# Retention and a gated MLP on one Trainium2 core: outputs of three chunks in two PSUM banks, a pair of first ups, other pieces of w_in, a w_out cast on GpSimd

## The chip, the core and the metric

One NeuronCore of a Trainium2 chip runs the whole kernel. The metric is device time in microseconds (us) of one execution; the number given is the median of several runs. Engines are named as the profile names them: PE is TensorE (matmuls), PEld its weight loads, DVE is VectorE, ACT is ScalarE, POOL is GpSimd, SP is SyncE, whose queue here only issues DMAs. Every engine works through its own instructions strictly in the order in which they are written; they wait for each other by semaphores.

## What is computed

```python
# q, k, v: 8 batches x 8 heads x 576 rows x 64, f32;  gamma of a head: 1 - 2^(-5-h)
scores = scale * q @ k.T                       # 576 x 576 per batch and head
ret = scores * where(i >= j, gamma**(i-j), 0)  # causal, decaying
attn = ret @ v                                 # retention, no softmax
x = attn.transpose(0, 2, 1, 3).reshape(4608, 512)
h = x @ w_in                                   # 512 x 2048
g = h * 1/(1 + exp(-beta*h))                   # beta per column of h
out = g @ w_out                                # 2048 x 512, f32
```

## The kernel before

**Retention in chunks.** The decay factors into a gain on q and a gain on k or v, so that rows are worked in chunks: 512 rows of a batch make four chunks of 128 (`seq[i]` gives batch and chunk; batch 0 has i = 0 to 3, batch 1 has 4 to 7), and the 64 rows left over in each batch are worked in pairs at four later places. For each chunk, in bf16: `pre_q` and `pre` scale and cast q, k and v (on DVE for the first two batches' q, else on POOL); `t_q` and `t_k` transpose them on PE through PSUM tiles `T` and copy them out (`qT`, `kT`); `a_sc` makes the scores of eight heads in two PSUM tiles `sc` and multiplies each by the causal mask on DVE (`R`); `a_O` multiplies `R` with v into the PSUM tile `O`; `a_cross` adds q times the state of the chunks before; `a_x` copies `O` to `xT`, the transposed input of the MLP; `a_st` adds the chunk's k^T v to the state `st` in PSUM and copies it out on ACT in two halves (`sbd`, or `end` after the last chunk). Below, "scores 6" or "T_k6" are those of chunk i = 6.

**The MLP.** A block is the 512 rows of a batch. `up(m, fo)` is four matmuls of 512 columns (one for each 128 rows of w_in, `ko`) into a PSUM tile `ph`, and ACT's Silu into `gT`; sixteen `fo` make a block. For block 1 the first ten are done in halves of 256 columns, since its chunks come two and two: first for chunks 4 and 5, then for 6 and 7. `down(m, ms, f0)` is four matmuls of a group of four `fo` for 128 rows `ms` into a PSUM tile `po`, copied out by DVE (`ot`) after the last group and stored.

**Loads and weights.** All loads stand in SP's queue: q of batch 0, k and v of its chunks, w_in in six pieces (four of 256 columns, two of 512), w_out in four groups, then q, k and v of batch 1, and so on. w_in pieces are cast to bf16 on DVE and POOL (L185, L186), w_out groups are scaled by 1/beta in three casts on DVE and one on ACT (L195 to L200). q of batch 1 arrives in two DMAs; `pre_q` makes four DVE instructions of it.

**Buffers.** PSUM has eight banks, given out by tag in turn: `mm` three (`ph`, `po`, the second `t_q`), `sc` two, `O` two (also `T`), `st` one. A tile waits until the one that had its bank has been read. For the fourth 128 rows of block 0, `po` takes the bank of the first rows' `po`, which the first `ot` copy releases.

**Order.** Nothing is scheduled by a compiler; the order of the program is each engine's order. Batch 0's chunks are written out by hand (L457 to L497). Then `merged` (L443) goes through `fill`, a list of ups and downs, and before unit n issues every step of `streams` whose due number is n or less. In block 0, `fill` has 16 ups, then (`d0` = 16) downs: twelve with `f0` outer and three `ms` inner, four for the last `ms`; `u1` = `d0` + 16 is block 1's first up. `second(i)` is `a_O` of two chunks, `a_cross` of both, `a_x` of both, and `a_st` of the second.

Of the kernel before, what the change touches and what calls it, by code (L numbers as in the profile page):

```python
# [19 lines left out]
def kernel(  # L20
# [110 lines left out]
    for h in range(H):  # L131
# [41 lines left out]
    def load_w_in(g):  # L173
        f0, fn = pieces[g]
        if f0 % 512 == 0:
            whole[0] = stage.tile([P, KO, 512], F32, name="wt", tag="wt", bufs=4)
        t = whole[0][:, :, f0 % 512:f0 % 512 + fn]
        nc.sync.dma_start(t, w_in_r[:, :, f0:f0 + fn])  # L178
        wts[g] = t

    def cast_w_in(g, kos=range(KO)):
        t = wts[g]
        f0, fn = pieces[g]
        for ko in kos:
            on_pool = ko == KO - 1 or g < 4 and ko > 1  # L185
            (nc.gpsimd if on_pool else nc.vector).tensor_copy(w_in_sb[:, ko, f0:f0 + fn], t[:, ko])  # L186
# [119 lines left out]
    def q_cols(i, r, p):  # L306

        b, c = seq[i]
        if b is None:
            return live[i]["qkT"][r, 0, p, :], lambda o: o  # L310
        return (batch[b]["qT"][r, :, p, c * PC:(c + 1) * PC], lambda o: o.rearrange("k (i s) -> k i s", i=CB))

    def a_sc(i):
        L = live[i]
        L["R"] = R = sb.tile([P, 2, HP, P], BF16, name="R", tag="R", bufs=4)

        tag = "mm" if i == CB - 1 else "O" if i >= E and (i - E) % 2 else "sc"
        sc = [psum.tile([P, HP, P], F32, name="sc", tag=tag, bufs=3 if tag == "mm" else 2) for _ in range(2)]
        for p in range(HP):
            for j in range(2):  # L320
                r = slice(j * D, (j + 1) * D)
                rhs, view = q_cols(i, r, p)
                nc.tensor.matmul(view(sc[j][:, p, :]), L["kT"][r, p, :], rhs, start=True, stop=True,  # L323
                                 skip_group_check=True)
        mask = causal if seq[i][0] is not None else causal2
        m_b = mask[:].unsqueeze(1).to_broadcast([P, HP, P])
        if i == CB - 1:

            half = sb.tile([P, HP, P], BF16, name="half", tag="half", bufs=1)
            nc.scalar.copy(half[:], sc[1][:])  # L330
            sc[1] = half
        for j in range(2):
            nc.vector.tensor_tensor(R[:, j], sc[j][:], causal4[:] if i == CB - 1 else m_b, ALU.mult)  # L333

    def a_cross(i, first):

        b, c = seq[i]
        L = live[i]
        if first:
            L["O"] = psum.tile([P, HP, P], F32, name="O", tag="O", bufs=2)  # L340
        if c == 0 and b is not None:
            return
        for p in range(HP):
            rhs, view = q_cols(i, slice(0, P), p)
            if b is None:
                for x in range(2):
                    r = slice(x * TL, (x + 1) * TL)
                    nc.tensor.matmul(L["O"][:, p, r], ends[(2 * c + x) % 4][:, p, :], rhs[:, r],
                                     start=False, stop=True, skip_group_check=True)
            else:  # L350
                nc.tensor.matmul(view(L["O"][:, p, :]), sbds[(c - 1) % NS][:, p, :], rhs,  # L351
                                 start=first and p == 0, stop=not first, skip_group_check=True)

    def a_O(i):

        b, c = seq[i]
        L = live[i]

        early = i < E
        if not early:  # L360
            tag = "sc" if b is not None and b >= QB and c > 1 else "O"
            L["O"] = psum.tile([P, HP, P], F32, name="O", tag=tag, bufs=2)
        O, R, vn = L["O"], L["R"], L["vn"]
        crossed = b is None or c > 0
        for j, p in [(n // HP, n % HP) if early else (n % 2, n // 2) for n in range(H)]:
            nc.tensor.matmul(O[j * D:(j + 1) * D, p, :], vn[:, 2 * p + j, :], R[:, j, p, :],  # L366
                             start=p == 0 and not (early and crossed), stop=early or not crossed,
                             skip_group_check=True)
        if early:
            a_x(i)  # L370

    def a_x(i):
        b, c = seq[i]
        O = live[i]["O"]
        if b is None:
            x = xt(B)[:, :, c, :]
        else:
            x, O = xt(b)[:, :, :, c * PC:(c + 1) * PC], O.rearrange("k p (i s) -> k p i s", i=CB)
        if i == CB - 1:
            nc.vector.tensor_copy(x[:, :2], O[:, :2])  # L380
            nc.scalar.copy(x[:, 2:], O[:, 2:])
        else:
            on_act = i < E or i % 2 == 0 if i < 2 * E else b is not None and c == 1
            (nc.scalar.copy if on_act else nc.vector.tensor_copy)(x, O[:])  # L384
# [21 lines left out]
    def up(m, fo, c0=0, cn=CB):  # L406
        if m not in gts:
            gts[m] = sb.tile([P, FO, CB, P], BF16, name="gT", tag="gT", bufs=2)
        w = slice(c0 * PC, (c0 + cn) * PC)
        ph = psum.tile([P, CB, P], F32, name="ph", tag="mm", bufs=3)  # L410
        ph = ph.rearrange("f i s -> f (i s)")[:, :cn * P].rearrange("f (i s) -> f i s", i=CB)
        for ko in range(KO):
            nc.tensor.matmul(ph, w_in_sb[:, ko, fo * P:(fo + 1) * P], xts[m][:, ko, :, w],  # L413
                             start=(ko == 0), stop=(ko == KO - 1))
# [38 lines left out]
    def F(f, *a):  # L453
        return lambda: f(*a)
# [66 lines left out]
    def second(i):  # L521
        for f in (a_O, lambda j: a_cross(j, False), a_x):
# [98 lines left out]
```

## Time and profile before

| what | value |
|---|---|
| runs | 311.74, 311.5, 311.76 us; median 311.74 |
| the profiled execution: time, span | 311.92 us, 310.1 us |
| granted TensorE clock | 0.998 of full speed |
| PE from 0 to 20 us | 15.29 us busy |
| PE from 20 to 40 us | 19.51 us busy |
| PE from 40 to 60 us | 19.15 us busy |
| PE from 60 to 250 us | 188.03 us busy |
| PE from 250 us to the end | 56.56 us busy; its last matmul ends at 306.8 |
| first up of block 0, first down, first up of block 1 | 19.48, 34.12, 52.22 us |
| w_in loads, 256 and 512 columns: issue to landing | 7.5 and 11.8 us |

The page of a profile gives busy time by engine, the span in 40 slices, DMA queues, the chain of work that ended last, and the costliest groups of instructions. A line of the timeline reads: start in us from the span's start, time covered, engine, source line, operation, out<-in by the program's names, shape, count, and in brackets how long the engine was idle before and what ended that. A run of equal instructions is merged into one line. A busy PE can still be waiting in part, as the ends of matmuls are modelled.

### The profile page before, as it was taken

Reading aid. Unit: us, or ns where it says so; the run is one execution under the profiler, and the core shown is the slowest. Engines: PE = TensorE matmul, PEld = TensorE weight load, DVE = VectorE, ACT = ScalarE, POOL = GpSimd, SP = SyncE. Lnnn points to the kernel's source line nnn. Section 1 sums busy time; section 2 is a strip of 40 time slices with the busy share of each in tenths; the row PEclk is TensorE's granted clock in tenths of the full one; section 3 lists DMA queues with packets and bytes.
Section 4 is the critical chain, followed back from the end, with each engine's and each line's share of the span. In section 5 each row is a group of like instructions: output and inputs, shape, how many; then the busy total and the mean of one; then the engine's idle time right before and its main releaser. Section 6 shows DMA issues by size and latency. Waiting matters only on the chain.

```text
span 310.1 us, 5363 instructions
## 1 busy us (share of the span) xinstructions
PE 298.5 (96%) x2144; PEld 157.8 (51%) x2177; DVE 106.9 (34%) x191; ACT 143.0 (46%) x256; POOL 96.0 (31%) x131
## 2 busy tenths in 40 slices
PE   7789999999999999999999999999999999999995
PEld 5544456775544454454554545455545444444444
DVE  7554476342531342434430434043405420010012
ACT  5567626995138412560186117711673037207700
POOL 4663026846524282254308031902420000000000
PEclk9999999999999999999999999999999999999999
DMA  8999999998989999999897697968852110031011
GB/s 207 221 355 387 380 232 273 233 257 179 202 197 162 224 189 235 218 212 198 133 234 107 136 205 207 201 115 192 196 76 37 68 70 0 17 88 34 0 70 68
DMA packets 123897, 52.79 MB, mean 170 GB/s; under 512 B 105680, under 2 KB 116320, under 8 KB 123872
## 3 DMA queue, kind: packets, MB, share of 16 engines
q1 hardware_dynamic: 98496, 46.15, 61.5%
q10 hardware_dynamic: 25376, 6.30, 13.6%
q8 instruction: 17, 0.28, 0.4%
q14 instruction: 8, 0.07, 0.1%
HBM read 36.71 MB, written 9.44 MB: 149 GB/s over the span
## 4 chain that ended last, share of the span: by engine, by line
PE 85%; DMA 6%; SPq 5%; DVE 1%; issue 1%; ACT 1%; POOL 1%; POOLq 0%
PE po L426 40%; PE ph L413 35%; DMA wt<-in_moe_w_in_dram 4%; SPq L94 3%; PE O L366 3%; PE sc L323 3%; DMA qn<-in_q_dram 2%; PE O L351 2%; PE st L396 2%; SPq L178 1%; POOL qs L247 1%; PE T L297 1%; PE T L303 1%; ACT gT L415 0%; DVE xT L384 0%
## 5 line engine op out<-in xcount | busy, mean ns | idle before, releaser
L415 ACT ACTIVATE gT<-ph,beta_sb 128x512 bf16<-128x512 f32 (+1 forms) x154 | 99.2, 659 | 86.3 <-PE ph L413 83.4
L413 PE MATMUL ph<-xT,w_in_sb 128*128 128x512 bf16 (+1 forms) x600 | 129.3, 365 | 3.2 <-DVE w_in_sb L186 0.9
L426 PE MATMUL po<-w_out_sb,gT 128*128 128x512 bf16 (+2 forms) x591 | 126.7, 368 | 1.1 <-issue 0.3
L413 PEld LDWEIGHTS <-w_in_sb 128*128 128x128 bf16 x616 | 58.7, 98 | 65.0 <-DVE w_in_sb L186 2.3
L426 PEld LDWEIGHTS <-gT 128*128 128x128 bf16 x608 | 57.1, 98 | 62.5
L333 DVE TENSOR_TENSOR R<-sc,causal 128x512 bf16<-128x512 f32 x71 | 44.3, 684 | 68.9 <-PE sc L323 68.9
L433 DVE COPY ot<-po 128x512 f32<-128x512 f32 (+2 forms) x38 | 25.0, 662 | 92.1 <-PE po L426 92.0
L255 POOL TENSOR_TENSOR vn<-kvn,gv 128x512 bf16<-128x512 f32 x32 | 33.4, 1042 | 22.8 <-DMA kvn<-in_v_dram 11.5
L247 POOL TENSOR_TENSOR qs<-qn,gq 128x512 bf16<-128x512 f32 x24 | 24.3, 1042 | 33.2 <-DMA qn<-in_q_dram 33.2
L273 POOL CAST kn<-kvn 128x512 bf16<-128x512 f32 x32 | 19.6, 612 | 47.7 <-DMA kvn<-in_k_dram 47.3
L401 ACT CAST sbd<-st 64x256 bf16<-64x256 f32 x48 | 17.4, 362 | 15.0 <-PE st L396 14.3
L384 DVE CAST xT<-O 128x512 bf16<-128x512 f32 x24 | 15.8, 688 | 19.6 <-PE O L366 9.6
L384 ACT CAST xT<-O 128x512 bf16<-128x512 f32 x11 | 6.4, 586 | 32.2 <-PE O L351 25.2
L396 PE MATMUL st<-vn,kn 128*128 128x128 bf16 x128 | 12.4, 219 | 0.2 <-POOL vn L255 0.2
L396 PEld LDWEIGHTS <-kn 128*128 128x128 bf16 x128 | 9.3, 98 | 5.0 <-issue 0.2
L366 PE MATMUL O<-R,vn 128*64 128x128 bf16 x288 | 10.7, 221 | 0.0
L323 PE MATMUL sc<-qT,kT 64*128 64x128 bf16 x256 | 10.3, 217 | 0.4 <-ACT kT L304 0.2
L366 PEld LDWEIGHTS <-vn 128*64 128x64 bf16 x288 | 8.5, 110 | 4.1 <-issue 3.6
L323 PEld LDWEIGHTS <-kT 64*128 64x128 bf16 x288 | 8.1, 94 | 3.8 <-ACT kT L304 1.5
L304 ACT COPY kT<-T 128x512 bf16<-128x512 bf16 x12 | 6.9, 586 | 4.8 <-PE T L303 4.8
L208 PE MATMUL ph<-warm 128*128 128x128 f32 (+1 forms) x24 | 7.0, 429 | 1.2 <-DVE warm L119 1.2
L186 DVE CAST w_in_sb<-wt 128x256 bf16<-128x256 f32 (+1 forms) x14 | 6.0, 476 | 5.2 <-DMA wt<-in_moe_w_in_dram 5.2
(56 smaller groups left out, 90.2 us busy)
## 6 DMA issues: line engine op xcount, KB each, us to landing
qn<-in_q_dram SPq DMA_DIRECT2D x16, 512.0 KB, 5.8
kvn<-in_k_dram SPq DMA_DIRECT2D x32, 256.0 KB, 5.9
kvn<-in_v_dram SPq DMA_DIRECT2D x32, 256.0 KB, 5.6
out_dram<-ot SPq DMA_DIRECT2D x31, 256.0 KB, 2.7
wt<-in_moe_w_out_dram SPq DMA_DIRECT2D x4, 1024.0 KB, 9.5
wt<-in_moe_w_in_dram SPq DMA_DIRECT2D x4, 512.0 KB, 7.5
wt<-in_moe_w_in_dram SPq DMA_DIRECT2D x2, 1024.0 KB, 11.8
out_dram<-ot SPq DMA_DIRECT2D x9, 128.0 KB, 2.4
```

The source lines that it names most:

```text
L247: e.tensor_tensor(batch[b]["qs"][:, cs, hs], q_tiles[b][:, hs, cs].rearrange("p h i d -> p i h d"), gq[:, cs, hs].unsqueeze(3).to_broadcas ...
L255: nc.gpsimd.tensor_tensor(live[i]["vn"][:], kv_tiles.pop(i)[:, 1], gains(gv, c), ALU.mult)
L273: nc.gpsimd.tensor_copy(kn[:, c % 2], t[:, 0])
L323: nc.tensor.matmul(view(sc[j][:, p, :]), L["kT"][r, p, :], rhs, start=True, stop=True, skip_group_check=True)
L333: nc.vector.tensor_tensor(R[:, j], sc[j][:], causal4[:] if i == CB - 1 else m_b, ALU.mult)
L366: nc.tensor.matmul(O[j * D:(j + 1) * D, p, :], vn[:, 2 * p + j, :], R[:, j, p, :], start=p == 0 and not (early and crossed), stop=early or ...
L384: (nc.scalar.copy if on_act else nc.vector.tensor_copy)(x, O[:])
L396: nc.tensor.matmul(st[:, p, :], heads(L["kn"], p), heads(L["vn"], p), start=(c == 0 and p == 0), stop=True, skip_group_check=True)
L413: nc.tensor.matmul(ph, w_in_sb[:, ko, fo * P:(fo + 1) * P], xts[m][:, ko, :, w], start=(ko == 0), stop=(ko == KO - 1))
L415: nc.scalar.activation(gts[m][:, fo, :, w], ph, ACT.Silu, scale=beta_sb[:, fo:fo + 1])
L426: nc.tensor.matmul(po[:, :nn], gT[:, fo, ms, :], w_out_sb[:, fo, n0:n0 + nn], start=(fo == 0), stop=(fo == FO - 1))
L433: nc.vector.tensor_copy(ot, po[:, :nn])
```

## The change

- **Two banks.** The output tiles of chunks 3, 5 and 7 become two tiles of half size (heads 0 to 3, heads 4 to 7), each in a bank of its own: chunk 3 in both `sc` banks, chunks 5 and 7 in one `O` and one `sc` bank. DVE copies the first half to `xT`, ACT the second. Before, chunk 3 was copied in halves out of one bank, and chunks 5 and 7 whole by DVE.
- **Chunk 3's products.** The ACT copy `half` of its second score tile goes, and so do `causal4` and its POOL copy; DVE multiplies both tiles from PSUM.
- **Order in batch 0.** `a_sc(3)` comes ahead of `a_cross(2)`, `a_x(1)` behind `t_k(3)`; `a_x` is called on its own.
- **Pieces of w_in.** Six of 256 columns and one of 512. Pieces 0, 1 and the last are loaded in two DMAs of two row groups each. Casts alternate between DVE and POOL by `ko`; in piece 0 POOL takes the first two; in the last piece the second two are cast 256 columns at a time.
- **First ups.** `up_pair` does `fo` 0 and 1 together: `ko` 0 and 1 of both, then `ko` 2 and 3 of each.
- **w_out.** The fourth cast of group 0 moves from ACT to POOL.
- **Due numbers.** Casts and loads of weights follow the new pieces; batch 1's transposes, scores, states and outputs have others.

```diff
-    causal4 = consts.tile([P, HP, P], BF16, name="causal4")
-    nc.gpsimd.tensor_copy(causal4[:], causal[:].unsqueeze(1).to_broadcast([P, HP, P]))
...
-    pieces = [(f, 256) for f in range(0, 1024, 256)] + [(f, 512) for f in range(1024, d_ff, 512)]
+    pieces = [(f, 256) for f in range(0, 1536, 256)] + [(f, 512) for f in range(1536, d_ff, 512)]
...
-        nc.sync.dma_start(t, w_in_r[:, :, f0:f0 + fn])
+        for w in (slice(0, 2), slice(2, KO)) if g in (0, 1, NP - 1) else (slice(0, KO),):
+            nc.sync.dma_start(t[:, w], w_in_r[:, w, f0:f0 + fn])
...
-            on_pool = ko == KO - 1 or g < 4 and ko > 1
-            (nc.gpsimd if on_pool else nc.vector).tensor_copy(w_in_sb[:, ko, f0:f0 + fn], t[:, ko])
+            on_pool = ko < 2 if g == 0 else ko % 2
+            e = nc.gpsimd if on_pool else nc.vector
+            if fn > 256 and ko == 2:
+                for x in range(0, fn, 256):
+                    for o, eng in ((2, nc.vector), (3, nc.gpsimd)):
+                        eng.tensor_copy(w_in_sb[:, o, f0 + x:f0 + x + 256], t[:, o, x:x + 256])
+            elif fn == 256 or ko < 2:
+                e.tensor_copy(w_in_sb[:, ko, f0:f0 + fn], t[:, ko])
...
-            if i == KO - 1:
+            if i == KO - 1 and g == 0:
+                nc.gpsimd.tensor_scalar(w_out_sb[:, fo, :], t[:, i], rbeta_sb[:, fo:fo + 1], None, ALU.mult)
+            elif i == KO - 1:
...
-        if i == CB - 1:
-
-            half = sb.tile([P, HP, P], BF16, name="half", tag="half", bufs=1)
-            nc.scalar.copy(half[:], sc[1][:])
-            sc[1] = half
         for j in range(2):
-            nc.vector.tensor_tensor(R[:, j], sc[j][:], causal4[:] if i == CB - 1 else m_b, ALU.mult)
+            nc.vector.tensor_tensor(R[:, j], sc[j][:], m_b, ALU.mult)
+
+    def split(i):
+        return i in (CB - 1, CB + 1, 2 * CB - 1)
+
+    def new_O(i):
+        b, c = seq[i]
+        if split(i):
+            tags = ("sc", "sc") if i == CB - 1 else ("O", "sc")
+            live[i]["O"] = [psum.tile([P, 2, P], F32, name="O", tag=t, bufs=2) for t in tags]
+        else:
+            tag = "sc" if b is not None and b >= QB and c > 1 else "O"
+            live[i]["O"] = [psum.tile([P, HP, P], F32, name="O", tag=tag, bufs=2)]
...
-        if i == CB - 1:
-            nc.vector.tensor_copy(x[:, :2], O[:, :2])
-            nc.scalar.copy(x[:, 2:], O[:, 2:])
+        Os = live[i]["O"]
+        if split(i):
+            nc.vector.tensor_copy(x[:, :2], view(Os[0]))
+            nc.scalar.copy(x[:, 2:], view(Os[1]))
         else:
-            on_act = i < E or i % 2 == 0 if i < 2 * E else b is not None and c == 1
-            (nc.scalar.copy if on_act else nc.vector.tensor_copy)(x, O[:])
+            on_act = i < 2 * E or b is not None and c == 1
+            (nc.scalar.copy if on_act else nc.vector.tensor_copy)(x, view(Os[0]))
...
+    def up_pair(m, fo, u):
...
+        fs = (fo, fo + 1)
+        if u == 0:
+            for f in fs:
+                phs[f] = psum.tile([P, MB], F32, name="ph", tag="mm", bufs=3)
+        for f, ko in [(f, ko) for ko in (0, 1) for f in fs] if u == 0 else [(f, ko) for f in fs for ko in (2, 3)]:
+            nc.tensor.matmul(phs[f][:], w_in_sb[:, ko, f * P:(f + 1) * P], xts[m][:, ko],
+                             start=(ko == 0), stop=(ko == KO - 1))
+            if ko == KO - 1:
+                nc.scalar.activation(gts[m][:, f], phs[f][:], ACT.Silu, scale=beta_sb[:, f:f + 1])
...
     t_k(3)
+    a_x(1)
     warm_up(1, 128)
+    a_sc(3)
     a_cross(2, True)
-    a_sc(3)
...
-    fill = [F(up, 0, fo) for fo in range(FO)]
+    fill = [F(up_pair, 0, fo, u) for fo in (0,) for u in range(2)] + [F(up, 0, fo) for fo in range(2, FO)]
...
-    streams = [[(0, F(load_w_out, 0)), (1.1, F(cast_w_in, 2)), (3.1, F(cast_w_in, 3)), (3.2, F(load_w_out, 1)),
-                (6.1, F(cast_w_in, 4)), (6.2, F(load_w_out, 2)), (10.1, F(cast_w_in, 5)), (10.2, F(load_w_out, 3))],
+    streams = [[(0, F(load_w_out, 0)), (0.1, F(cast_w_in, 2)), (2.1, F(cast_w_in, 3)), (2.2, F(load_w_out, 1)),
+                (4.1, F(cast_w_in, 4)), (6.1, F(cast_w_in, 5)), (6.2, F(load_w_out, 2)), (8.1, F(cast_w_in, 6)),
+                (8.2, F(load_w_out, 3))],
...
-               [(d0 + 7, F(pre_q, 1, n)) for n in range(4)] + [(d0 + 10.6, F(t_q, 1, 0)), (d0 + 12.6, F(t_q, 1, 1))],
+               [(d0 + 7, F(pre_q, 1, n)) for n in range(4)] + [(d0 + 11.6, F(t_q, 1, 0)), (d0 + 12.6, F(t_q, 1, 1))],
...
-                (d0 + 12.7, F(t_k, 4)), (d0 + 12.8, F(t_k, 5)), (d0 + 13.8, F(a_sc, 4)), (d0 + 13.81, F(a_sc, 5)),
-                (d0 + 14.8, F(a_st, 4)), (d0 + 15.9, F(second, 4))],
+                (d0 + 12.7, F(t_k, 4)), (d0 + 14, F(t_k, 5)), (d0 + 14, F(a_sc, 4)), (d0 + 15, F(a_sc, 5)),
+                (d0 + 15.7, F(a_st, 4)), (d0 + 15.9, F(second, 4))],
...
-                (d0 + 15.8, F(t_k, 6)), (d0 + 15.91, F(t_k, 7)), (u1 + 1.8, F(a_sc, 6)), (u1 + 1.81, F(a_sc, 7)),
-                (u1 + 2.8, F(a_st, 6)), (u1 + 8.8, F(second, 6))]]
+                (d0 + 15.95, F(t_k, 6)), (u1 + 1, F(t_k, 7)), (u1 + 3, F(a_sc, 6)), (u1 + 3.01, F(a_sc, 7)),
+                (u1 + 4, F(a_st, 6)), (u1 + 8.8, F(second, 6))]]
```

More of the change, by code (lines that the diff above doesn't have):

```diff
@@ L326, in a_sc, with O_of, opens @@
         m_b = mask[:].unsqueeze(1).to_broadcast([P, HP, P])
-        if i == CB - 1:
-            half = sb.tile([P, HP, P], BF16, name="half", tag="half", bufs=1)
-            nc.scalar.copy(half[:], sc[1][:])
-            sc[1] = half
         for j in range(2):
-            nc.vector.tensor_tensor(R[:, j], sc[j][:], causal4[:] if i == CB - 1 else m_b, ALU.mult)
+            nc.vector.tensor_tensor(R[:, j], sc[j][:], m_b, ALU.mult)
[9 more added lines that the diff above has]
+            live[i]["O"] = [psum.tile([P, HP, P], F32, name="O", tag=tag, bufs=2)]
+    def O_of(i, p):
+        Os = live[i]["O"]
+        return Os[p // 2][:, p % 2] if split(i) else Os[0][:, p]
+    def opens(i, p):
+        return p == 0 or split(i) and p == 2
     def a_cross(i, first):
         b, c = seq[i]
-        L = live[i]
         if first:
-            L["O"] = psum.tile([P, HP, P], F32, name="O", tag="O", bufs=2)
+            new_O(i)
         if c == 0 and b is not None:
@@ L344, in a_cross @@
             rhs, view = q_cols(i, slice(0, P), p)
+            O = O_of(i, p)
             if b is None:
@@ L347, in a_cross @@
                     r = slice(x * TL, (x + 1) * TL)
-                    nc.tensor.matmul(L["O"][:, p, r], ends[(2 * c + x) % 4][:, p, :], rhs[:, r],
+                    nc.tensor.matmul(O[:, r], ends[(2 * c + x) % 4][:, p, :], rhs[:, r],
                                      start=False, stop=True, skip_group_check=True)
             else:
-                nc.tensor.matmul(view(L["O"][:, p, :]), sbds[(c - 1) % NS][:, p, :], rhs,
-                                 start=first and p == 0, stop=not first, skip_group_check=True)
+                nc.tensor.matmul(view(O), sbds[(c - 1) % NS][:, p, :], rhs,
+                                 start=first and opens(i, p), stop=not first, skip_group_check=True)
     def a_O(i):
@@ L360, in a_O @@
         if not early:
-            tag = "sc" if b is not None and b >= QB and c > 1 else "O"
-            L["O"] = psum.tile([P, HP, P], F32, name="O", tag=tag, bufs=2)
-        O, R, vn = L["O"], L["R"], L["vn"]
+            new_O(i)
+        R, vn = L["R"], L["vn"]
         crossed = b is None or c > 0
         for j, p in [(n // HP, n % HP) if early else (n % 2, n // 2) for n in range(H)]:
-            nc.tensor.matmul(O[j * D:(j + 1) * D, p, :], vn[:, 2 * p + j, :], R[:, j, p, :],
-                             start=p == 0 and not (early and crossed), stop=early or not crossed,
+            nc.tensor.matmul(O_of(i, p)[j * D:(j + 1) * D], vn[:, 2 * p + j, :], R[:, j, p, :],
+                             start=opens(i, p) and not (early and crossed), stop=early or not crossed,
                              skip_group_check=True)
-        if early:
-            a_x(i)
     def a_x(i):
         b, c = seq[i]
-        O = live[i]["O"]
         if b is None:
-            x = xt(B)[:, :, c, :]
+            x, view = xt(B)[:, :, c, :], lambda o: o
         else:
-            x, O = xt(b)[:, :, :, c * PC:(c + 1) * PC], O.rearrange("k p (i s) -> k p i s", i=CB)
-        if i == CB - 1:
-            nc.vector.tensor_copy(x[:, :2], O[:, :2])
-            nc.scalar.copy(x[:, 2:], O[:, 2:])
-        else:
-            on_act = i < E or i % 2 == 0 if i < 2 * E else b is not None and c == 1
-            (nc.scalar.copy if on_act else nc.vector.tensor_copy)(x, O[:])
+            x, view = xt(b)[:, :, :, c * PC:(c + 1) * PC], lambda o: o.rearrange("k p (i s) -> k p i s", i=CB)
+        Os = live[i]["O"]
+        if split(i):
+            nc.vector.tensor_copy(x[:, :2], view(Os[0]))
+            nc.scalar.copy(x[:, 2:], view(Os[1]))
+        else:
+            on_act = i < 2 * E or b is not None and c == 1
+            (nc.scalar.copy if on_act else nc.vector.tensor_copy)(x, view(Os[0]))
     def a_st(i):
@@ L415, in up @@
         nc.scalar.activation(gts[m][:, fo, :, w], ph, ACT.Silu, scale=beta_sb[:, fo:fo + 1])
+    phs = {}
+    def up_pair(m, fo, u):
+        if m not in gts:
+            gts[m] = sb.tile([P, FO, CB, P], BF16, name="gT", tag="gT", bufs=2)
+        fs = (fo, fo + 1)
[7 more added lines that the diff above has]
+                nc.scalar.activation(gts[m][:, f], phs[f][:], ACT.Silu, scale=beta_sb[:, f:f + 1])
     pos_, ots = {}, {}
@@ L474 @@
     a_O(0)
+    a_x(0)
     a_sc(1)
@@ L489 @@
     a_O(2)
+    a_x(2)
     pre(3, (1,))
@@ L493 @@
     a_O(3)
+    a_x(3)
     cast_w_in(0)
```

## Prediction

> **What bounds it now.** I read the page first (busy time, slices), then the timeline from 12 to 66 us, the weights' tiles, and the waits.
>
> ```profile
> span 310.1 us, 5363 instructions
> PE 298.5 (96%) x2144; PEld 157.8 (51%) x2177; DVE 106.9 (34%) x191; ACT 143.0 (46%) x256; POOL 96.0 (31%) x131
> PE   7789999999999999999999999999999999999995
> ACT  5567626995138412560186117711673037207700
> ```
>
> TensorE is busy in all but the first three slices and the last. The diff touches what runs up to about 60 us; past that no instruction changes its place. So the sum is: when does TensorE, now, reach the uninterrupted stretch that begins at 59.44, and when after the change. The waits it could lose there are small; the timeline shows how they hang on loads and on ScalarE:
>
> ```profile
> 18.88 0.80 POOL L186 CAST w_in_sb<-wt 128x256 bf16<-128x256 f32 x2 [1.75 <-DMA wt<-in_moe_w_in_dram]
> 20.35 0.70 DVE L186 CAST w_in_sb<-wt 128x256 bf16<-128x256 f32 x2 [0.53 <-DMA wt<-in_moe_w_in_dram]
> ...
> 26.06 1.51 DVE L186 CAST w_in_sb<-wt 128x512 bf16<-128x512 f32 x3 [2.02 <-DMA wt<-in_moe_w_in_dram]
> ...
> 28.77 1.51 DVE L186 CAST w_in_sb<-wt 128x512 bf16<-128x512 f32 x3 [1.20 <-DMA wt<-in_moe_w_in_dram]
> ...
> 42.66 1.29 DVE L247 TENSOR_TENSOR qs<-qn,gq 128x512 bf16<-128x512 f32 x2 [0.27 <-DMA qn<-in_q_dram]
> ...
> 43.88 1.94 DVE L433 COPY ot<-po 128x512 f32<-128x512 f32 x3
> ...
> 44.06 1.89 PE L426 MATMUL po<-w_out_sb,gT 128*128 128x512 bf16 x8
> ```
>
> To see: every cast starts when its piece lands. A 256-wide piece (512 KB, 1 KB packets) takes 20.35 - 18.88, about 1.49 us; a 512-wide one (1 MB, 2 KB packets) 28.77 - 26.06 = 2.71. Through all of this the slices show the DMA engines at 9 tenths. VectorE's third qs waits for q of batch 1 to land, and the ot copies stand behind qs in VectorE's order.
>
> **Up to 44 us: a gain.** Chunk 3's kT copy goes ahead of x(1) on ScalarE: its transposes end at 14.99, so 15.03 to 15.62 instead of 15.37 to 15.97, and chunk 3's scores start at 15.67 (now 16.02). `half` goes: ScalarE loses 0.58, VectorE's second product reads PSUM, 0.69 instead of 0.41; both products end at 17.41 (now 17.55). Without `half` the state copies run 16.65 to 17.41 (now to 17.72), so the cross product starts at 17.46 instead of 17.77 and everything to chunk 3's output is 0.31 earlier. Its two halves (0.42 on DVE, 0.37 on ACT, one after the other now, 18.59 to 19.42) lie in two banks and run together: 18.28 to 18.70. The first row half of piece 0 lands half a piece earlier, 18.13; GpSimd's two casts (0.4 each) are done by 18.95. First up matmul: 18.76 instead of 19.48. The pair's order needs rows 2 and 3 only at the fifth matmul, so the 0.2 us wait inside the first up goes, and with 256-wide pieces the 0.6 us wait at 26.5 to 27.6 goes. 64 matmuls x 0.216 = 13.82: down starts at 32.6 (now 34.12).
>
> Against it, one 512-wide piece becomes two 256-wide: 2 x 1.49 - 2.71 = **0.27 us later** for every load behind it. Four more DMAs: taken as nothing (the engines never run dry); at most 0.1 from the spread of the 1.49s. w_out then lands at 31.7, 34.4, 37.1, 39.8; its casts cost some 0.4 us of waits in twelve units of 4 x 0.216 = 0.863. GpSimd's w_out cast has no row: bounds 0.61 (its bf16 cast of this size) and 1.04 (its product); I take 0.87, the w_in cast of the same shape. It is wanted at 33.2, lands 31.7, so it is hidden either way; uncovered it costs at most 0.4. Taking its share from ScalarE (0.72) frees nothing that TensorE waits for. With T_q's 0.45 TensorE reaches the first unit of the fourth 128 rows at 43.8, 1.1 us before today's 44.92.
>
> The Trainium skill (GPSIMD Engine Reference, Key points) speaks against GpSimd here: elementwise work is about 2x faster on VectorE, and the two share SBUF interfaces. The rows agree in kind: of the three 128x512 casts from 26.06 on, VectorE's second takes 0.84 beside GpSimd's and its third 0.41 alone. By it VectorE's first w_out casts are 0.4 us later; that falls into the 1.1 us above.
>
> **At 44 us: the gain is lost.** That unit takes the PSUM buffer of the first rows' po, released by the first ot copy, which VectorE does after the fourth qs, whose load lands 0.27 later: 42.93; two qs 0.61 apart, ot 44.14 to 44.83, TensorE at 44.88. Now: ot ends 44.56, TensorE arrives at 44.92. **Net 0.04 earlier**; all the rest of the 1.1 is a new wait there.
>
> **From 44.9 to 61: a loss.**
>
> ```profile
> 49.54 0.76 ACT L401 CAST sbd<-st 64x256 bf16<-64x256 f32 x2 [1.81 <-PE st L396]
> ...
> 50.57 0.58 ACT L304 COPY kT<-T 128x512 bf16<-128x512 bf16 x1 [0.27 <-PE T L303]
> ...
> 51.06 0.59 ACT L384 CAST xT<-O 128x512 bf16<-128x512 f32 x1
> ...
> 51.47 0.69 DVE L384 CAST xT<-O 128x512 bf16<-128x512 f32 x1 [0.32 <-PE O L351]
> ...
> 51.75 0.76 ACT L401 CAST sbd<-st 64x256 bf16<-64x256 f32 x2
> ...
> 52.22 0.77 PEld L413 LDWEIGHTS <-w_in_sb 128*128 128x128 bf16 x8 [0.51 <-DVE xT L384]
> ...
> 52.53 0.58 ACT L304 COPY kT<-T 128x512 bf16<-128x512 bf16 x1
> ...
> 53.20 0.45 PEld L323 LDWEIGHTS <-kT 64*128 64x128 bf16 x16 [0.21 <-issue]
> ```
>
> To see: today ScalarE does chunk 4's state copies and chunk 6's kT while TensorE still has down units; x5 on VectorE costs the weight loads 0.5 us of idle at 52.22. The change puts a_st(4) after the last down unit (15.7 for 14.8), chunk 6's transposes behind second(4), chunk 7's behind an up unit (its buffer is x5's new bank), and half of x5 on ScalarE. From 44.92, with today's durations: T_q to 46.23, T_k4 to 46.45, unit, T_k5 to 47.54, scores 4 at 47.63, unit, scores 5 at 48.92, unit to 50.10, st4, O4 50.43, O5 50.72 (VectorE's products of chunk 5 end 50.65). State copies start 0.48 after st4, as now: 50.58 to 51.34, and chunk 5's cross product, queued on TensorE in front of st5, T_k6 and all ups, waits for them until 51.39 (now 51.04). Then x5's half on DVE 51.82 to 52.24: first up at 52.30 (now 52.22), the split's 0.3 already in it.
> ScalarE then has, in order and by today's spacings: state copies 50.58, x4 51.36, half x5 51.84, state copies 52.11, kT6 52.89, first gT 53.37, kT7 53.74 to 54.33. Chunk 6's scores need kT7's buffer back: 54.42, against 53.20 now with one half up (0.44) less in front. TensorE idles 0.6 there, another 0.24 for a PSUM buffer at the eighth half up, where today's 0.3 at 56.07 goes. O6 starts at 58.31 (now 57.47): +0.84. Splitting x7 gives 0.26 back: the up behind it at 60.02 (now 59.44): **+0.58**. But its ScalarE half pushes the end-state copies and the next gT to 60.82 to 61.29, so the up three on waits from 60.89 to 61.34: **+0.45**, and the backlog is gone. Sum -0.04 + 0.58 + 0.45 = **+1.0**. The stall at 165.2 (q load behind an out store) moves along unchanged.
>
> On the profiled execution's own 311.92 (span 310.1, 1.8 around it) that is 312.9; on the median of the runs, 311.74, it is **312.7**.
>
> **Rivals.**
> 1. *The clamp at 44 us opens* (q lands early enough). The DMA view from 15.5 to 18.9 has one 16 KB instruction packet with 2.6% of 16 engines, 1.4 us on one engine; the first w_in piece's other engines report by 17.5, that one at 18.83, and it stays last until 42.6. If it fell elsewhere, q would land up to 1.1 us sooner, TensorE go on at 43.8: -1.1 + 1.0, **311.7**. Against: the instruction stream is nearly the same. By the Trainium skill (Runtime: NRT & Kernel Launch, Instruction fetch mechanics) such a 16 KiB refill is mostly hidden; by that this rival would be the forecast; the row says it isn't.
> 2. *Faster: the ScalarE chain is shorter than I queue it.* The clamp stays, but its copies overlap, so that neither cross 5 nor scores 6 wait; then the splits take the idle at 52.2, 56.1 and 59.4: 0.3 + 0.2 + 0.2 = -0.7, **311.0**. Deciding point: kT7 done before the third half up ends (53.8). For: ACT rows do overlap by 0.1; against: seven copies sum to 3.8 us from st4.
> 3. *The same, half as bad*: one of the two ScalarE waits does not appear, +0.3, **312.0**.
> 4. *Worse*: q lands 0.7 or more later than reckoned (the packet delays a second engine), **313.5**.
>
> **Chances.** Forecast 0.50, rivals 0.09, 0.22, 0.11, 0.08. About 0.2% (0.62 us) is what can be told from no change: slower 0.58, same 0.20, faster 0.22. The range takes in rivals 1 to 3 and the bounds of the casts and loads: 311.0 to 313.5.
>
> **What would show it.** Right: first up near 18.8, down near 32.6, an idle TensorE of about 1 us near 43.8 ended by VectorE's ot; state copies of chunk 4 near 50.6; idle of 0.6 before scores 6, ended by ScalarE's kT; ups past x7 near 60.0. Wrong: q's qs before 42.5, kT7 before 53.8, or down not starting before 33.5 (then the wait at 44 is smaller, the total not).

## The result and the profile after

The changed kernel takes 312.29 us (median of 20 runs), the kernel before 311.6 in the same comparison: ratio 1.0025, 95% interval 1.0013 to 1.0037. By the ratio that is **0.78 us slower** (0.40 to 1.15); the two medians differ by 0.69. The profiled execution took 312.14 us, with a span of 310.4.

The page after, the same lines as were shown of before:

```profile
span 310.4 us, 5377 instructions
PE 299.4 (96%) x2144; PEld 158.0 (51%) x2177; DVE 106.1 (34%) x192; ACT 142.6 (46%) x256; POOL 100.0 (32%) x136
PE   7799999999999999999999999999999999999996
ACT  5577426896127511670177116721574037306700
```

At this grain only the third slice shows a thing: TensorE has less idle time at 16 to 23 us. The rest is in the timeline. The w_in casts and the first stretch of w_out (columns: start, time covered, engine, line, operation, what, shape, count, idle before):

```profile
17.02 0.74 POOL L190 CAST w_in_sb<-wt 128x256 bf16<-128x256 f32 x2
...
31.86 1.71 DVE L206 TENSOR_SCALAR w_out_sb<-wt,rbeta_sb 128x512 bf16<-128x512 f32 x3 [2.08 <-DMA wt<-in_moe_w_out_dram]
31.93 2.11 POOL L202 TENSOR_SCALAR w_out_sb<-wt,rbeta_sb 128x512 bf16<-128x512 f32 x1 [1.90 <-DMA wt<-in_moe_w_out_dram]
...
32.63 0.38 PE L459 MATMUL po<-w_out_sb,gT 128*128 128x512 bf16 x1
...
33.23 2.96 PE L459 MATMUL po<-w_out_sb,gT 128*128 128x512 bf16 x11 [0.22 <-DVE w_out_sb L206]
```

Down starts at 32.63, 1.5 us earlier than before, as predicted. GpSimd's w_out cast takes 2.11 us and ends at 34.04; the fourth matmul, which reads it, starts at 34.09 and could have started at about 33.3. That and VectorE's slower casts put holes of 0.39, 0.18 and 0.25 us between the first four matmuls. Then, at 44 us:

```profile
42.97 1.29 DVE L253 TENSOR_TENSOR qs<-qn,gq 128x512 bf16<-128x512 f32 x2 [0.28 <-DMA qn<-in_q_dram]
...
43.80 0.61 PE L303 MATMUL T<-ident,qs 128*128 128x128 bf16 x8
...
44.17 1.88 DVE L466 COPY ot<-po 128x512 f32<-128x512 f32 x3
...
44.91 1.02 PE L459 MATMUL po<-w_out_sb,gT 128*128 128x512 bf16 x4 [0.50 <-DVE ot L466]
```

TensorE's eight transposes take 0.45 us from start to start, so it could go on at 44.25. It waits until 44.91, 0.66 us, for the first ot copy, which stands behind two qs, which wait for q. The fourth 128 rows start at 44.91; before it was 44.92. All that was won is gone. Behind it:

```profile
50.61 0.76 ACT L418 CAST sbd<-st 64x256 bf16<-64x256 f32 x2 [2.29 <-PE st L413]
...
51.39 0.59 ACT L401 CAST xT<-O 128x512 bf16<-128x512 f32 x1
...
51.42 0.40 PE L371 MATMUL O<-qT,sbd 128*128 128x128 bf16 x4 [0.31 <-ACT sbd L418]
...
51.74 0.42 DVE L397 CAST xT<-O 128x256 bf16<-128x256 f32 x1 [0.50 <-PE O L371]
...
51.87 0.38 ACT L398 CAST xT<-O 128x256 bf16<-128x256 f32 x1
...
53.77 0.59 ACT L310 COPY kT<-T 128x512 bf16<-128x512 bf16 x1
...
54.41 0.38 PE L329 MATMUL sc<-qT,kT 64*128 64x128 bf16 x7 [0.32 <-ACT kT L310]
```

The state copies start late (they used to start at 49.54), chunk 5's cross product waits for them, ScalarE's copies stand one behind the other up to 54.36, and chunk 6's scores wait for the last of them. Behind chunk 7's output one more wait, in a later stretch of the same timeline:

```profile
59.84 0.38 ACT L398 CAST xT<-O 128x256 bf16<-128x256 f32 x1
60.11 0.75 ACT L418 CAST end<-st 64x256 bf16<-64x256 f32 x2
...
61.41 0.82 PE L430 MATMUL ph<-xT,w_in_sb 128*128 128x256 bf16 x6 [0.32 <-ACT gT L432]
```

Batch 2's first transposes of q come at 63.15 (before: 62.07), 1.08 us later, and from there on no instruction has another place.

### The profile page after: what moved, and what is told of

It reads as the page before. It is cut to its first block, busy times and chain, and to the rows that moved or that the text cites. A ratio compares the mean times of both kernels' runs of the same rounds, so it can differ in the third digit from the quotient of the medians.

```text
span 310.4 us, 5377 instructions
## 1 busy us (share of the span) xinstructions
PE 299.4 (96%) x2144; PEld 158.0 (51%) x2177; DVE 106.1 (34%) x192; ACT 142.6 (46%) x256; POOL 100.0 (32%) x136
## 4 chain that ended last, share of the span: by engine, by line
PE 78%; DMA 8%; SPq 7%; ACT 2%; issue 1%; POOL 1%; DVE 1%; ACTq 0%; POOLq 0%
PE po L459 37%; PE ph L430 32%; DMA qn<-in_q_dram 6%; SPq L94 3%; PE sc L329 3%; DMA wt<-in_moe_w_in_dram 3%; SPq L176 3%; PE O L385 3%; PE st L413 2%; PE O L371 2%; POOL qs L253 1%; ACT gT L432 1%; SPq L81 1%; DVE ot L466 1%; PE T L309 0%
## 5 line engine op out<-in xcount | busy, mean ns | idle before, releaser
L432 ACT ACTIVATE gT<-ph,beta_sb 128x512 bf16<-128x512 f32 (+1 forms) x152 | 97.9, 660 | 84.7 <-PE ph L430 83.4
L430 PE MATMUL ph<-xT,w_in_sb 128*128 128x512 bf16 (+1 forms) x593 | 127.4, 365 | 1.5 <-ACT gT L432 0.7
L430 PEld LDWEIGHTS <-w_in_sb 128*128 128x128 bf16 x608 | 58.0, 98 | 62.0 <-issue 1.4
L334 DVE TENSOR_TENSOR R<-sc,causal 128x512 bf16<-128x512 f32 x72 | 45.0, 684 | 69.4 <-PE sc L329 68.2
L279 POOL CAST kn<-kvn 128x512 bf16<-128x512 f32 x32 | 19.6, 614 | 44.9 <-DMA kvn<-in_k_dram 44.3
L401 DVE CAST xT<-O 128x512 bf16<-128x512 f32 x22 | 14.5, 688 | 16.6 <-PE O L385 9.7
L190 POOL CAST w_in_sb<-wt 128x256 bf16<-128x256 f32 (+1 forms) x13 | 6.4, 510 | 4.5 <-DMA wt<-in_moe_w_in_dram 4.5
```

The costliest lines, as they stand in the source:

```text
L279: nc.gpsimd.tensor_copy(kn[:, c % 2], t[:, 0])
L334: nc.vector.tensor_tensor(R[:, j], sc[j][:], m_b, ALU.mult)
L401: (nc.scalar.copy if on_act else nc.vector.tensor_copy)(x, view(Os[0]))
```

## A yardstick

Spans of single executions can't be compared to 0.3 us here. Four kernels below have the loads of before; in their traces the third qs (where q of batch 1 lands) starts at 42.66, 42.72, 42.81 and 43.23, and the last matmul ends 243.87 to 244.86 us behind batch 2's first transposes. What does repeat, to some 0.03, is the distance between events that hang on each other. So every trace is read by four distances:

- **loads**: how much later q lands than in before, measured from the casts of the fourth w_in piece, which both have alike: 23.34 to 42.66 before, 23.36 to 42.97 after, so 0.29 us (0.28 to 0.31 in the other traces with these loads, but for two; see below the table);
- **clamp**: from the start of the third qs to the second transposes of q (the `T` of heads 4 to 7);
- **stretch**: from there to batch 2's first transposes of q;
- **end**: from the end of the last matmul to the end of the span.

Their sum against before is what a trace says of a kernel, and the timed runs say it independently. For the changed kernel: 0.29 - 0.32 + 1.09 - 0.43 = +0.63, measured +0.78.

| kernel | loads | clamp | stretch | end | sum against before | measured against before, us (95%) |
|---|---|---|---|---|---|---|
| before | - | 3.12 | 16.29 | 3.32 | - | - |
| changed | +0.29 | 2.80 | 17.38 | 2.89 | +0.63 | +0.78 (0.40 to 1.15) |
| e1_due | +0.29 | 2.81 | 16.49 | 2.90 | -0.24 | +0.16 (-0.25 to 0.53) |
| e2_nosplit | +0.29 | 2.81 | 17.17 | 2.89 | +0.43 | +0.69 (0.22 to 1.15) |
| e3_up | +0.29 | 2.81 | 16.29 | 2.89 | -0.45 | -0.34 (-0.81 to 0.12) |
| e4_down | 0 | 3.12 | 17.37 | 3.32 | +1.08 | +1.28 (0.90 to 1.65) |
| e5_ot_first | +1.06 | 1.94 | 17.37 | 2.90 | +0.54 | -0.12 (-0.81 to 0.53) |
| e9_ot_act | +0.53 | 1.88 | 16.61 | 2.90 | -0.81 | -1.34 (-1.96 to -0.72) |
| e8_pool5 | 0 | 3.14 | 16.29 | 3.39 | +0.09 | 0.0 (-0.65 to 0.65) |
| e11_due45 | +0.29 | 2.81 | 16.86 | 2.89 | +0.12 | +0.03 (-0.56 to 0.65) |
| b2_before_ot | 0 | 3.12 | 16.29 | 3.32 | 0.0 | +0.03 (-0.50 to 0.56) |
| b1_act_cast | +0.29 | 2.75 | 16.29 | 3.34 | -0.06 | -0.12 (-0.69 to 0.44) |
| b5_best | +0.29 | 2.75 | 16.51 | 3.33 | +0.15 | +0.28 (-0.34 to 0.90) |
| e10_after_ot_act | +0.29 | 2.13 | 17.38 | 2.89 | -0.04 | 0.0 (-0.53 to 0.56) |

(Measured: the ratio to before in that comparison, less one, times 311.6.) Every sum lies in its interval but e5_ot_first's, which is 0.01 outside. In e5_ot_first the third qs starts late because it stands behind a copy, and q itself landed some 0.5 us later than in the others; in e9_ot_act q landed 0.25 later. One trace each can't tell whether that belongs to the kernel or to the execution.

## The experiments

**Which half makes the loss.** Four kernels take the change apart. The due numbers of batch 1 put back:

```diff
-               [(d0 + 7, F(pre_q, 1, n)) for n in range(4)] + [(d0 + 11.6, F(t_q, 1, 0)), (d0 + 12.6, F(t_q, 1, 1))],
+               [(d0 + 7, F(pre_q, 1, n)) for n in range(4)] + [(d0 + 10.6, F(t_q, 1, 0)), (d0 + 12.6, F(t_q, 1, 1))],
...
-                (d0 + 12.7, F(t_k, 4)), (d0 + 14, F(t_k, 5)), (d0 + 14, F(a_sc, 4)), (d0 + 15, F(a_sc, 5)),
-                (d0 + 15.7, F(a_st, 4)), (d0 + 15.9, F(second, 4))],
+                (d0 + 12.7, F(t_k, 4)), (d0 + 12.8, F(t_k, 5)), (d0 + 13.8, F(a_sc, 4)), (d0 + 13.81, F(a_sc, 5)),
+                (d0 + 14.8, F(a_st, 4)), (d0 + 15.9, F(second, 4))],
...
-                (d0 + 15.95, F(t_k, 6)), (u1 + 1, F(t_k, 7)), (u1 + 3, F(a_sc, 6)), (u1 + 3.01, F(a_sc, 7)),
-                (u1 + 4, F(a_st, 6)), (u1 + 8.8, F(second, 6))]]
+                (d0 + 15.8, F(t_k, 6)), (d0 + 15.91, F(t_k, 7)), (u1 + 1.8, F(a_sc, 6)), (u1 + 1.81, F(a_sc, 7)),
+                (u1 + 2.8, F(a_st, 6)), (u1 + 8.8, F(second, 6))]]
```

> The changed kernel with the due numbers of before for batch 1's transposes, scores, states and outputs; the two-bank outputs, the pair of first ups, the pieces of w_in and the GpSimd cast stay. Theory A (mine: upstream gain ends at the first ot copy, near 44.9, and the loss is made behind it by the new due numbers, on ScalarE's order): the cross product of chunk 5 is back at about 51.04, the first half-up comes at about 51.9 with the split copies, chunk 6's output at about 57.5; 0.4 to 0.7 us faster than before. Theory B (the loss is made upstream: 0.27 us later loads, the added DMAs, GpSimd's 2.11 us cast of w_out): still 0.5 to 0.9 us slower than before. Theory C (the split of 5 and 7, which puts a copy on ScalarE among the Silus, makes the loss): 0.5 to 1.0 slower than before.

Measured ratio 1.0005 (0.9992 to 1.0017); against the changed kernel about 0.6 us are back. No theory had the number. Theory A's first half held, its second did not: the first half-up comes 0.38 us sooner behind the second transposes of q than in e3_up, as the split of chunk 5 should make it, but the half copy on ScalarE puts chunk 7's kT later, and chunk 6's scores wait for that: chunk 6's output starts 11.69 us behind those transposes, 11.68 in e3_up. Nothing is left of the gain, and the stretch ends up 0.20 longer than without the splits.

Only chunk 3 split, all else as changed:

```diff
-        return i in (CB - 1, CB + 1, 2 * CB - 1)
+        return i == CB - 1
...
-            on_act = i < 2 * E or b is not None and c == 1
+            on_act = i < E or i % 2 == 0 if i < 2 * E else b is not None and c == 1
```

> The changed kernel with only chunk 3's output in two banks; the outputs of chunks 5 and 7 are whole again and copied by VectorE. Due numbers and all else as changed. Theory A: first half-up some 0.3 us later than in the changed kernel, chunk 7's ups some 0.26 later: 0.2 to 0.6 us slower than the changed kernel, 1.0 to 1.4 slower than before. Theory B: as the changed kernel, within 0.2. Theory C: as before, within 0.2.

Measured 1.0022 (1.0007 to 1.0037): the loss is there without the splits of 5 and 7, so theory C falls; theory A's 0.2 to 0.6 on top are not there either (stretch 17.17 against 17.38): the two splits cost 0.2 with either set of due numbers. All but 0.02 of it comes behind chunk 6's output, from the split of chunk 7, whose ScalarE half stands ahead of the Silus. First e1_due, which has the wait of the changed kernel's 61.41, then e2_nosplit, which has none:

```profile
60.89 1.91 PE L430 MATMUL ph<-xT,w_in_sb 128*128 128x256 bf16 x16 [0.32 <-ACT gT L432]
...
59.58 3.52 PE L430 MATMUL ph<-xT,w_in_sb 128*128 128x256 bf16 x28
```

Theory B's number came (0.20 apart), but not for its reason, as the next run shows. Both edits together:

> The upstream half of the change alone: order in batch 0, chunk 3 in two banks, pair of first ups, pieces of w_in, GpSimd cast. Chunks 5 and 7 whole and the due numbers of batch 1 as before. Theory A: the fourth 128 rows' first unit starts at 44.9 as before, and everything behind it as before: within 0.2 us of before. Theory B: all of the loss, 0.6 to 0.9 us slower than before. Theory C: within 0.2 of before, but then the kernel with only the due numbers put back is slow.

Measured 0.9989 (0.9974 to 1.0004). Theory B falls: the upstream half loses nothing. Its stretch is the 16.29 of before, and the first row of its waits (columns: who waited for whom, us in total, times, longest) has the clamp in it:

```profile
PE po L459 <- DVE ot L466: 0.5, 1, 0.5
PE ph L430 <- DVE xT L401: 0.3, 1, 0.3
PE ph L430 <- ACT gT L432: 0.2, 1, 0.2
```

The other half alone, with batch 0, w_in, first ups and w_out as before:

> The downstream half alone: batch 0, w_in, first ups and w_out casts as before; chunks 5 and 7 in two banks and the new due numbers of batch 1. Theory A: the fourth 128 rows' first unit at 44.9, chunk 6's output at about 58.3, 0.6 to 1.0 us slower than before, as the changed kernel is. Theory B: within 0.2 us of before. Theory C: 0.6 to 1.0 slower than before.

Measured 1.0041 (1.0029 to 1.0053), the stretch 17.37. So the loss is made behind 44.9, and mostly by the due numbers: 0.88 of the 1.09 us (e2_nosplit), the rest by the splits. What the upstream half takes off it, 0.45 us by the four distances, is nearly all the shorter end; up to the second transposes of q it wins 0.02. To see which due numbers, e2_nosplit with those of chunks 6 and 7 put back:

> The changed kernel with chunks 5 and 7 whole and chunk 6's and 7's due numbers as before, so that of the new due numbers only those of q and of chunks 4 and 5 are left. Theory A: the cross product of chunk 5 waits 0.3 us for ScalarE's state copy, as in the changed kernel, but the wait of 0.32 us before chunk 6's scores is gone; between the upstream half (311.1) and the kernel with all new due numbers and no split (311.9), at 311.3 to 311.7. Theory G (one of the two groups carries all of it): at one of the two ends.

Measured 1.0001 (0.9982 to 1.0021), too wide to decide by itself; the stretch is 16.86. Of the 0.88 us that the due numbers add (17.17 - 16.29), 0.57 is due to those of q and chunks 4 and 5, 0.31 to those of chunks 6 and 7. Theory G falls by the trace. Theory A's 0.3 us wait for the state copy is not there as a wait, since chunk 6's transposes fill it, but chunk 5's cross product comes as late as in the changed kernel: 5.65 us behind the second transposes of q, against 5.25 in before.

**The clamp.** The third and fourth qs behind the first ot copy:

```diff
-               [(d0 + 7, F(pre_q, 1, n)) for n in range(4)] + ...
+               [(d0 + (7 if n < 2 else 9.5), F(pre_q, 1, n)) for n in range(4)] + ...
```

> The changed kernel with one move: VectorE's third and fourth qs of batch 1 come behind the first ot copy instead of ahead of it. Theory A (TensorE's gain ends at the first ot copy, which stands behind the third qs, which waits for q to land): the wait of 0.50 us at 44.9 goes, the fourth 128 rows start at about 44.2, chunk 6's output at about 57.7; 0.5 to 0.9 us faster than the changed kernel, so within 0.3 of before. Theory D (the loads are the bound: k and v of batch 1 land when they land, and TensorE waits for the next of them instead): less than 0.2 us faster than the changed kernel, and a new wait of the same size before the transposes of chunk 5 or 6.

Measured 0.9996 (0.9974 to 1.0017) to before, where the changed kernel has 1.0025. The wait at 44.9 is gone, but a shorter one, 0.28 us, stands a unit later, again for an ot: the second transposes of q take the buffer of the second rows' po, whose copy now stands behind the qs. In this execution q landed latest of all, at about 43.6 (the third qs, behind the ot copy, starts at 43.88), and still the second transposes came at 45.82, against 45.77 in the changed kernel. No new wait stands before the transposes of chunk 5 or 6, so theory D falls; theory A's 0.5 to 0.9 us agree with the timed runs (0.9, from two comparisons), but this one trace can't show them.

The copies taken off VectorE altogether, in e3_up:

```diff
-        nc.vector.tensor_copy(ot, po[:, :nn])
+        (nc.scalar.copy if m == 0 and ms < 3 else nc.vector.tensor_copy)(ot, po[:, :nn])
```

> The upstream half alone (chunks 5 and 7 whole, batch 1's due numbers as before), with the first three ot copies of block 0 on ScalarE, which is idle there, instead of VectorE. Theory A: no wait for ot; the fourth 128 rows and the second transposes of q 0.5 to 0.9 us earlier than in the upstream half; then chunk 5's transposes wait for its kn cast, so that 0.3 to 0.8 us are left: 310.3 to 310.9 us, faster than before by 0.6 to 1.2. Theory D: as the upstream half, 311.0 to 311.3.

Measured 0.9957 (0.9937 to 0.9977), 310.8 us where before had 311.87: **the fastest of all, faster than both kernels**. Its timeline:

```profile
42.59 0.59 ACT L466 COPY ot<-po 128x512 f32<-128x512 f32 x1 [1.44 <-DMA kvn<-in_k_dram]
...
43.50 1.29 DVE L253 TENSOR_TENSOR qs<-qn,gq 128x512 bf16<-128x512 f32 x2 [0.28 <-DMA qn<-in_q_dram]
...
43.66 1.89 PE L459 MATMUL po<-w_out_sb,gT 128*128 128x512 bf16 x8
...
45.38 0.61 PE L303 MATMUL T<-ident,qs 128*128 128x128 bf16 x8
...
46.36 0.23 PEld L309 LDWEIGHTS <-kn 128*128 128x128 bf16 x4 [0.32 <-POOL kn L279]
```

The first ot copy runs while q is still landing, eight matmuls go through without a hole, and the next wait is chunk 5's kn cast, 0.32 us, as theory A said. The same edit in before, where TensorE had no wait at that place:

> The kernel before with one edit: the first three ot copies of block 0 on ScalarE instead of VectorE. Theory A (the ot copies on VectorE only hold the kernel up once TensorE comes earlier than before, as it does with the new upstream half): TensorE had no wait there, nothing changes: within 0.3 us of before. Theory H (the gain of the kernel with the new upstream half and these copies on ScalarE, 1.3 us, comes from the copies alone): 0.6 to 1.3 us faster than before.

Measured 1.0001 (0.9984 to 1.0018), all four distances as before. Theory H falls: the copies on ScalarE pay only where TensorE comes early. And in the changed kernel, complete:

> The changed kernel, complete, with only the first three ot copies of block 0 on ScalarE. Theory A: the wait at 44.9 goes and TensorE starts the fourth 128 rows up to 0.7 us earlier, but from there to the first transposes of batch 2's q it needs the same 18.2 us as in the changed kernel, 1.1 more than in before: 0.4 to 0.8 us faster than the changed kernel, so within 0.4 us of before. Theory K (the long way from there on is only the late start's doing): under 17.5 us for that stretch, and 0.8 us or more faster than before.

Measured 1.0000 (0.9983 to 1.0018). Stretch 17.38, the changed kernel's: theory K falls, the late start had no part in it. The waits from 42 us on:

```profile
PE sc L329 <- ACT kT L310: 0.3, 1, 0.3
PE ph L430 <- ACT gT L432: 0.3, 1, 0.3
PE O L371 <- ACT sbd L418: 0.3, 1, 0.3
```

The last is the due numbers' doing: e2_nosplit has it, e1_due has not. The second is that of chunk 7's split, shown above. The first is ScalarE's queue, which the due numbers make late: the second matmul of chunk 6's scores comes 8.64 us behind the second transposes of q here, 8.62 in e2_nosplit (where the later first half-up covers most of the wait) and 7.44 in e1_due.

**GpSimd's cast.** e9_ot_act with the fourth w_out cast of group 0 on ScalarE again:

```diff
-            if i == KO - 1 and g == 0:
-                nc.gpsimd.tensor_scalar(w_out_sb[:, fo, :], t[:, i], rbeta_sb[:, fo:fo + 1], None, ALU.mult)
-            elif i == KO - 1:
+            if i == KO - 1:
```

> The upstream half with the first three ot copies on ScalarE, and the fourth w_out cast of group 0 back on ScalarE as in before, so that only this cast's engine differs from the run with the copies on ScalarE. Theory A (GpSimd's cast takes 2.11 us and ends 1.2 us behind the moment TensorE needs it, now no longer covered): the waits at about 33.5 shrink, TensorE comes up to 0.8 us earlier to the transposes of q, but batch 1's q and k then land too late, so that 0 to 0.4 us are left. Theory I (the cast on GpSimd keeps ScalarE free for the last Silus and is worth having): slower by 0.2 to 0.7 us than with GpSimd's cast.

Measured 0.9996 (0.9978 to 1.0014), 311.81 us: the two runs are from two comparisons, with the intervals just apart. Theory I holds, by the traces a little above what it said; 0.44 of the 0.75 us by which the sums differ is the end (below), and the rest comes about like this:

```profile
31.84 0.72 ACT L202 ACTIVATE w_out_sb<-wt,rbeta_sb 128x512 bf16<-128x512 f32 x1 [1.53 <-DMA wt<-in_moe_w_out_dram]
31.85 1.28 DVE L204 TENSOR_SCALAR w_out_sb<-wt,rbeta_sb 128x512 bf16<-128x512 f32 x3 [2.08 <-DMA wt<-in_moe_w_out_dram]
32.46 2.47 ACT L430 ACTIVATE gT<-ph,beta_sb 128x512 bf16<-128x512 f32 x4
33.18 1.02 PE L428 MATMUL ph<-xT,w_in_sb 128*128 128x512 bf16 x4 [1.01 <-ACT gT L430]
...
34.04 2.32 PE L457 MATMUL po<-w_out_sb,gT 128*128 128x512 bf16 x10
```

On ScalarE the cast stands ahead of four Silus and waits 1.53 us for w_out to land; TensorE waits 1.01 us for a Silu to give back its PSUM buffer, and down starts at 34.04 instead of 32.9. GpSimd's slow cast costs less than ScalarE's stuck queue. On top of it, with chunk 5's transposes behind the second unit:

```diff
-                (d0 + 12.7, F(t_k, 4)), (d0 + 12.8, F(t_k, 5)), (d0 + 13.8, F(a_sc, 4)), (d0 + 13.81, F(a_sc, 5)),
+                (d0 + 12.7, F(t_k, 4)), (d0 + 13.5, F(t_k, 5)), (d0 + 13.8, F(a_sc, 4)), (d0 + 14.5, F(a_sc, 5)),
```

> The kernel with the w_out cast back on ScalarE, with chunk 5's transposes put behind the second unit of the fourth 128 rows and its scores behind the third, so that TensorE has work while chunk 5's kn is cast. Theory A: the wait for kn before chunk 5's transposes (0.3 us in the run with the ot copies on ScalarE) goes: 0.1 to 0.4 us faster than without this move, the fastest of all, 310.2 to 310.7 where before is 311.5. Theory J (chunk 5's products then come late for its output): as slow or slower than without this move, with a wait of TensorE for R before chunk 5's output.

Measured 1.0009 (0.9989 to 1.0029), and the stretch is 16.51, 0.22 longer: a miss. With the cast on ScalarE there was no wait for kn left to hide. The loss stands already at chunk 5's cross product (5.47 us behind the second transposes of q, 5.25 without the move), and no wait for R is there: theory J has the direction, not the reason. It was tried on the wrong base; on e9_ot_act it was not tried.

**The end.** In every kernel with the whole new upstream half, 0.43 us of the time behind the last matmul is gone. Was it GpSimd's instruction count?

```diff
     nc.gpsimd.memset(causal2[:TL, TL:], 0.0)
+    for _ in range(5):
+        nc.gpsimd.memset(causal2[:TL, TL:], 0.0)
```

> The kernel before with five more GpSimd instructions (136 in all, as in the changed kernel): the small memset of the second mask's corner five times over, at about 21 us, where GpSimd waits for loads. Theory E (the 0.43 us by which the end behind the last matmul is shorter in all kernels with the new upstream half comes from where GpSimd's program ends, since its next to last semaphore instruction stands 0.36 us in before and 0.07 in the changed kernel): the stretch behind the last matmul is 2.9 us instead of 3.3, 0.2 to 0.5 us faster than before. Theory F (it comes from another engine's program or from the last store): within 0.15 of before, 3.3 us behind the last matmul.

Measured 1.0000 (0.9979 to 1.0021), end 3.39. Theory E falls. But b1_act_cast and b5_best, which have all of the upstream half except GpSimd's w_out cast, also have the long end (3.34, 3.33): the 0.43 goes with that one instruction's move from ScalarE to GpSimd. The pair that differs in nothing else, b1_act_cast and then e9_ot_act (the last matmul ends at 306.69 and 306.83):

```profile
core 0 of [0], span 310.0 us
298.68 8.01 PE L457 MATMUL po<-w_out_sb,gT 128*128 128x512 bf16 x68
...
core 0 of [0], span 309.7 us
298.82 8.01 PE L459 MATMUL po<-w_out_sb,gT 128*128 128x512 bf16 x68
```

By what means stays open, and the move alone, in before, was not tried.

## Why the prediction was right, and where it was not

312.7 was predicted (311.0 to 313.5), 312.29 measured; as a change, +0.96 predicted, +0.78 measured (0.40 to 1.15). Up to batch 2's first transposes, which is what the sum was about, it has +0.99 and the trace +1.06. The steps:

- **Up to 44 us: right in kind, one term too small.** First up 18.81 (said 18.76), down 32.63 (32.6), loads later by 0.29 (0.27). The waits for w_out casts were 0.82 us, not 0.4, so TensorE came to the fourth 128 rows at 44.25, not at 43.8, and the wait that was to be "about 1 us" was 0.66. The first row half was cast at 17.02 in this execution, not at 18.13; in seven others with these loads it was at 18.1 to 18.5. Here the first up waited for chunk 3's output and not for it.
- **The clamp: right**, 44.91 (44.88), net gain 0.00 to 0.04 (0.04), in all five traces with every qs ahead of the ot copies on VectorE. It swallowed the 0.45 us above as well, as the prediction's last paragraph says of a late down. Rival 1 never came up: by e10_after_ot_act an open clamp is worth 0.7 us, not 1.1, since TensorE came later than reckoned.
- **The loss behind it: right.** Stretch +1.09 (1.0): state copies 50.61 (50.58), cross product 51.42 (51.39), first half-up 52.23 (52.30), scores 54.41 (54.42), O6 58.36 (58.31), third wait 61.41 (61.34). (Chunk 6's first score matmul came at 53.87, the others at 54.41.) Neither ScalarE wait was spared, so rivals 2 and 3 did not come.
- **"I take 0.87, the w_in cast of the same shape" for GpSimd's w_out cast: wrong**, 2.11 us, and outside the bounds of 0.61 to 1.04 that the two nearest rows gave. It was not "hidden either way": with VectorE's slowed casts it made the 0.82 us of waits, where the sum had 0.4; the clamp covered the rest. The groups of the w_out tile, after (count: shortest, median and longest, in ns):

```profile
L206 DVE TENSOR_SCALAR w_out_sb<-wt,rbeta_sb x12: 474/482/918, 31.9 to 40.7; 128x512 bf16<-128x512 f32 x12
L204 ACT ACTIVATE w_out_sb<-wt,rbeta_sb x3: 721/722/723, 34.6 to 39.9; 128x512 bf16<-128x512 f32 x3
L202 POOL TENSOR_SCALAR w_out_sb<-wt,rbeta_sb x1: 2107/2107/2107, 31.9 to 31.9; 128x512 bf16<-128x512 f32 x1
```

  VectorE's longest, 918 ns, is the one in the middle of GpSimd's; without it (b1_act_cast) all three are 481 to 486. The Trainium skill (SBUF — State Buffer, SBUF: two separate sides) says that the two engines share a pair of ports under an exclusive lock, held for a whole instruction, if VectorE's instruction is in a two-port mode or has two SBUF inputs. Whether these casts are of that kind, no run here shows. The trace agrees that GpSimd's cast slows one of VectorE's, but not that it shuts VectorE out: all three were done by 33.57, and GpSimd's one runs from 31.93 to 34.04. What GpSimd's takes with VectorE idle was not tried, so how much of the 2.11 us is the neighbour's doing stays open.
- **"Taking its share from ScalarE (0.72) frees nothing that TensorE waits for": wrong.** b1_act_cast shows 1.0 us of wait at 33.18 for it. The step looked at the 0.72 us of work and not at the load that the cast waits for in the order of ScalarE's queue. In the changed kernel this gain went the way of the others at 44 us, so the sum did not notice.
- **Nothing was said of the end**: -0.43 us in the trace (2.89 for 3.32). With it the trace has +0.63 in all, and the timed +0.78 lies between that and the forecast. That the total came so near owes something to this: without the end it would have been slightly above the forecast instead of below.
- **"The stall at 165.2 (q load behind an out store) moves along unchanged": wrong in cause and size.** It was 0.77 us before and 0.51 after; elsewhere it was 0 to 1.1, see below. It is an accident of each execution and, with 0.12 us at 124 us in before, explains why the two profiled spans differ by only 0.3 where the four distances give 0.63.

## What to carry over

Gains ahead of a copy that stands, in its engine's order, behind a wait for a load are worth what the load gives, until the copy is taken out of that order. Read how far each step stands from the landing it hangs on, not from the start: these distances repeated to some 0.03 us where the spans scatter by 1. Ask of a copy on a shared in-order engine what stands ahead of it and what that waits for: three copies moved to an idle engine took back here all that the whole change had lost (e10_after_ot_act). Steps put later to make room for an engine make a queue on the next one, and the last of the queue is what waits.

## Not expected of the hardware

The wait near 165 us is ScalarE's own queue. There it issues a transposing DMA (ACTq: the issuing). The timeline of before:

```profile
162.17 2.29 ACTq L281 DMA_TRANSPOSE kT<-kn  x1
...
165.24 1.02 PE L413 MATMUL ph<-xT,w_in_sb 128*128 128x512 bf16 x4 [0.60 <-ACT gT L415]
```

And of e4_down, where the issue is short and the matmuls run on:

```profile
161.83 5.34 PE L435 MATMUL ph<-xT,w_in_sb 128*128 128x512 bf16 x24
...
163.19 1.26 ACTq L281 DMA_TRANSPOSE kT<-kn  x1
```

The issue holds up the Silus behind it, and its time varies from trace to trace, though that part of the program does not: 1.25 to 2.63 us at this place. From start to start, TensorE's loss there is the issue's time less 1.52 us: 0.77 at 2.29 (before), 0.52 at 2.03 (after), 0.74 at 2.26, 1.12 at 2.63, 0.26 at 1.78, none at 1.25 and 1.26. Another such issue at 124 us took 1.7 to 3.2 us and cost up to 0.98, its time less 2.20. These two make the scatter behind batch 2's first transposes: from there to the last matmul's end the 14 traces have 243.87 to 245.39 us, and with the two losses taken off 243.86 to 243.88. What makes an issue long, no run here shows.
